# Seven products for one of four first-layer column groups in blocks 3 to 6 of a retention and MLP kernel, with x sums on GpSimd

## The chip, the cores and the metric

The kernel runs on one core of a Trainium2 chip. The metric is the device time of one execution in microseconds (us). A profiled execution gives a trace beside its time: its span is the time between its first and last instruction. Engines are called PE (matmuls), ACT, DVE, POOL (GpSimd) and SP, whose queue issues most DMAs here.

## The reference

For 8 batches of 8 heads, 576 positions and head size 64, the kernel computes a retention layer and then a two-layer MLP on all 4608 tokens.

```python
scores = scale * q @ k.T                       # per batch and head
ret = scores * where(rel >= 0, gamma[h] ** rel, 0)
x = (ret @ v)  ->  [4608, 512]                 # heads side by side
h = x @ w_in                                   # 512 -> 2048
g = gelu_tanh(h)
out = g @ w_out                                # 2048 -> 512, float32
```

## The kernel before, in words

**Tiling.** The MLP runs in nine blocks of 512 tokens: block t (0 to 7) is the first 512 positions of batch t, and block 8 holds the last 64 positions ("tails") of all batches. Each block has a first layer (512 to 2048 columns, hidden chunks f = 0 to 15 of 128 each) and a second layer. While block t runs, pieces of the retention of batch t+1 are placed between its matmuls, and batch t+2 is loaded and cast.

**First layer.** In most blocks it is sixteen calls of `up` (L474): four matmuls of 128x512 (L480) fill one PSUM bank `hp`, and ACT writes its gelu to `gT` in float16 (L486). `act_sums` (L634) then forms, on DVE, the sums s1, s2, s4 and an in-place difference of parts of `gT`; they are the left sides of the second layer.

**Second layer.** It is always done by Strassen and Winograd's scheme: seven half-size products (`prod`, L648), each in two halves of eight 128x256 matmuls, in the order 1, 6, 5, 7, 2, 4, 3. Products 6, 7 and 4 add to one bank `opB`. `after` (L672) takes the results out: product 1 by an ACT copy (s1, tag k1), product 6 by a DVE add (u2, tag k2), product 7 by another (u3, tag k3). Product 7 may write `opB` only when the u2 add has read it.

**Seven products in the first layer.** In blocks 7 and 8 (`WIN`), three of four column groups of the first layer are done in the same way by `up_prod` (L554): group j holds the hidden chunks 2j, 2j+1, 8+2j and 9+2j, and seven products of four 128x256 matmuls (L574) replace four `up`. Products 1, 6, 7 and 4 add up in one bank hB, 5 and 3 in hC, 2 goes to hA. Between them the partial sum of hB is copied out: after product 1 by ACT (L594), after product 6 by ACT (L600), after product 7 by DVE (L602). DVE adds hA or hC to the copies (L581), and ACT takes the gelu of the sums; that gelu is recorded after the next product or `up`. The sums of weights come from `in_sums` (L518) and those of x from `x_sums` (L535), all on DVE, the latter kept in x12 and x34. Their tiles take places of the loads' ring.

**What sets the order.** Everything is emitted in program order; `at(t, u, f)` places a piece of work f behind step u (0 to 29) of block t. Steps 0 to 15 are the first layer; 16 to 29 are the fourteen halves of the second. In blocks 2 to 6 the scores of chunks 0 and 1 of the next batch (and of tails, where there are any) are at step 11 or 9, the outputs `outs` of those chunks at 15, of chunks 2 and 3 at 24. `outs` ends in `state` (L402), which multiplies the casts of k and v of chunks 0 and 1 of the batch after, and in `put` (L466), the ACT copy to xT. `later` (L784) is a DVE scan and a `spread` (L430), two ACT copies of 64x256; two of them stand at the start of each block.

**Loads.** `pump` issues loads in a fixed list on SP as buffers of one ring of 16 come free; a mark in the list holds it until `resume` at step 29. A batch is twelve loads of 256 KB, in the order k, q, v for chunks 0 to 3, followed by six tail loads (two each for k, q and v) for batches 4, 5 and 7. From step 16 the casts are placed: k and q on POOL (L275), v on ACT (L262) or, for batch 3, POOL. `gate` (L979), a one-element POOL copy that reads the last s4, stands ahead of them. One step behind the casts stand two DMA transposes of k and q (L308) and, with tails, two POOL casts and one more transpose (`cast_tails`, L245).

Of the kernel before, what the change touches and what calls it, by code (L numbers as in the profile page):

```python
# [20 lines left out]
def kernel(  # L21
# [23 lines left out]
    LD = 16  # L45
# [3 lines left out]
    NT4 = 4  # L49
    scale = 1.0 / math.sqrt(D)  # L50
# [18 lines left out]

    def lds():  # L70
        return sb.tile([128, 512], F32, tag="ld", name="ld", bufs=LD)

# [66 lines left out]
    q_ld = {"next": 0, "free": LD, "hold": False}  # L139

    def pump(freed=0):
        q_ld["free"] += freed
        while q_ld["next"] < len(seq) and not q_ld["hold"]:
            s = seq[q_ld["next"]]
            if s[0] == "h":
                q_ld["hold"] = True
                q_ld["next"] += 1
                return
            if s[0] != "t":
                if q_ld["free"] == 0:  # L150
                    return
                q_ld["free"] -= 1
            q_ld["next"] += 1
            {"b": load, "i": load_w_in, "o": load_w_out, "t": load_tails}[s[0]](*s[1:])
# [101 lines left out]
    def cast(b, key, c, eng):  # L256
        a = att[b]
        raw = a["raw"].pop((key, c))
        dst = a[key][:, 512 * c : 512 * c + 512]
        if key == "v":  # L260
            if eng is nc.scalar:
                eng.copy(out=dst, in_=raw)  # L262
            else:
                eng.tensor_copy(out=dst, in_=raw)
        elif b < NPE:
            y = c % 2
            eng.tensor_tensor(
                out=a[key][:, 1024 * (c // 2) : 1024 * (c // 2) + 1024].rearrange("p (n l d) -> p l n d", l=2, d=D)[:, y],
                in0=raw.rearrange("p (n d) -> p n d", d=D),
                in1=sp[key][:, :, y].unsqueeze(2).to_broadcast([128, 8, D]),  # L270
                op=ALU.mult,
            )
        else:
            s0 = {"q": 0, "k": 2}[key] + (b >= PAIR)
            eng.tensor_tensor(  # L275
                out=dst.rearrange("p (h d) -> p h d", d=D),
                in0=raw.rearrange("p (h d) -> p h d", d=D),
                in1=sc[:, s0].unsqueeze(2).to_broadcast([128, 8, D]),
                op=ALU.mult,
            )  # L280
# [233 lines left out]
    WIN = {t: 3 for t in (NTB - 2, NTB - 1)}  # L514
    GW = max(WIN.values())
    wi = {}

    def in_sums(j, ns):  # L518
        if not wi:
            for g in range(0, GW, 2):  # L520
                for n in "234":
                    wi[n, g // 2] = sb.tile([128, 2, 512], F16, tag="ld", name="wi" + n, bufs=LD)
# [12 lines left out]
    def x_sums(t):  # L535
        if not xw:
            for n in ("12", "34"):
                x = sb.tile([128, 2, 4, 2, TL], F16, tag="ld", name="x" + n, bufs=LD)
                xw[int(n[0])], xw[int(n[1])] = x[:, 0], x[:, 1]
            for n in range(3):  # L540
                for s in "svu" if n < 2 else "vu":
                    wk[s, n] = sb.tile([128, 512], F32, tag="ld", name="w" + s, bufs=LD)
# [3 lines left out]
        for s, x, y, f in (  # L546
# [3 lines left out]
            nc.vector.tensor_tensor(out=s, in0=x, in1=y, op=f)  # L550

    wk, wb, due = {}, {}, []

    def up_prod(t, j, m):  # L554
# [23 lines left out]
        s, v, u3 = wk["s", j % 2], wk["v", j % 3], wk["u", j % 3]  # L578
# [55 lines left out]
    def act_sums(t, f0, f1, us=slice(0, 2), parts=(0, 1)):  # L634
# [6 lines left out]
        if 0 in parts:  # L641
            nc.vector.tensor_tensor(out=s["1"], in0=a21, in1=a22, op=ALU.add)  # L642
            nc.vector.tensor_tensor(out=s["2"], in0=s["1"], in1=a11, op=ALU.subtract)
            nc.vector.tensor_tensor(out=a21, in0=a11, in1=a21, op=ALU.subtract)  # L644
        if 1 in parts:
            nc.vector.tensor_tensor(out=s["4"], in0=a12, in1=s["2"], op=ALU.subtract)  # L646
# [25 lines left out]
    def after(t, m, u):  # L672
# [87 lines left out]
    def cast_w(kind, *i):  # L760
# [11 lines left out]
        pump(1)  # L772
# [4 lines left out]
    def cc(b, key, c, eng):  # L777
        cast(b, key, c, eng)
        pump(1)
# [135 lines left out]
    for t, b in TP.items():  # L915
        at(t, 3, lambda b=b: tail_values(b))
# [30 lines left out]
    for t in range(1, B):  # L947
        b, tl = t + 1, TP.get(t)
        s0, o0, s1, o1 = U2 if t == 1 else (11 if t in (2, 3) else 9, 15, 15, 24)
# [6 lines left out]
        else:  # L956
            at(t, s1, lambda b=b: (score(b, 2), score(b, 3)))
            at(t, 17, lambda b=b: masks(b, 2))
            at(t, 19, lambda b=b: masks(b, 3))
# [7 lines left out]
    for b in range(NPE, B):  # L967
# [23 lines left out]
    for t in range(NTB):  # L991
# [9 lines left out]
        else:  # L1001
# [7 lines left out]
            todo = deque(f + h for f in range(2 * WIN.get(t, 0), NH) for h in (0, NH))  # L1009
            for w in (W_ORDER if t in WIN else ()):  # L1010
# [7 lines left out]
                def token(w):  # L1018
# [5 lines left out]
                    elif w[0] in "ab":  # L1024
                        act_sums(t, 2 * int(w[1]), 2 * int(w[1]) + 2, parts=("ab".index(w[0]),))
                    else:
                        up_prod(t, int(w[0]), int(w[1]))
                steps.append((mixed, 0 if w[:1] in ("a", "b", "Q") else 1 if w else 2))
            for f in range(0 if t == 1 or t in WIN else NH):
# [55 lines left out]
```

## Time and profile before

| what | us |
|---|---|
| median of three runs (lowest to highest) | 293.72 (293.19 to 295.14) |
| profiled execution, time and span | 293.76 and 292.0 |
| start of blocks 2, 3, 4, 5, 6, 7 on PE | 84.43, 114.70, 145.15, 175.60, 205.37, 236.00 |
| PE busy in block 4 (145.15 to 175.60) | 30.45 of 30.45 |
| DVE, ACT and POOL busy in block 4 | 18.92, 18.84, 9.11 |
| PE busy over the span | 280.1 |

A row of a timeline reads: start in us, duration in us, engine, line, operation, output and inputs with their shape and type, how many in a row; the bracket is the idle time of the engine ahead of it, and what ended that. A row of the chain of waits reads: start, duration, engine, output, line. The granted clock of PE was 1.00 in each of these blocks.

### The profile page before, as it was taken

What the parts mean: (1) busy time and instruction counts of PE and PEld (TensorE: products, weight loads), DVE (VectorE), ACT (ScalarE), POOL (GpSimd) and SP (SyncE); (2) the same over time, 40 slices, a digit from 0 to 9 for tenths busy, and PEclk for the clock granted to TensorE, in tenths of its full rate; (3) what the DMA queues carried; (4) which work ended last, traced back from release to release, by engine and by line L of the source; (5) the groups of instructions that cost most, each with busy time, mean ns of one, the idle gap of its engine ahead of it and who ended that gap; (6) DMA issues with size and microseconds to landing.
All of it is one profiled execution on the core that took longest, in us unless ns stands there. A gap on an engine that the chain in (4) does not pass through costs nothing.

```text
span 292.0 us, 7383 instructions
## 1 busy us (share of the span) xinstructions
PE 280.1 (96%) x3024; PEld 207.6 (71%) x3024; DVE 204.1 (70%) x409; ACT 169.8 (58%) x321; POOL 100.0 (34%) x128
## 2 busy tenths in 40 slices
PE   6889998999999999999999999999999999999993
PEld 2558877888874687468845884488548887887783
DVE  7796998666864874477548834784489968974863
ACT  5487754987249545964396647664666258507810
POOL 4589779910661175008500730068030000000000
PEclk9999999999999999999999999999999999999998
DMA  6999999989999999999999979997952030003013
GB/s 195 308 382 370 364 293 228 252 213 163 225 192 230 235 206 183 244 235 210 200 267 209 218 147 270 216 190 99 271 95 38 2 144 3 0 21 125 3 36 108
DMA packets 139585, 53.95 MB, mean 185 GB/s; under 512 B 118048, under 2 KB 131360, under 8 KB 139552
## 3 DMA queue, kind: packets, MB, share of 16 engines
q1 hardware_dynamic: 138960, 52.97, 80.4%
q8 instruction: 23, 0.38, 0.6%
q10 hardware_dynamic: 592, 0.52, 0.5%
q14 instruction: 10, 0.08, 0.1%
HBM read 36.70 MB, written 9.44 MB: 158 GB/s over the span
## 4 chain that ended last, share of the span: by engine, by line
PE 66%; SPq 8%; DMA 8%; ACT 5%; POOL 5%; DVE 5%; issue 1%; POOLq 0%; DVEq 0%; ACTq 0%
PE hp L480 18%; PE opB L665 11%; PE opA L665 8%; PE opC L665 7%; SPq L101 5%; DMA ld<-in_moe_w_in_dram 4%; PE hp L501 4%; PE hB L574 3%; SPq L96 3%; ACT gT L486 3%; PE xs L459 2%; POOL w_out_sb L771 2%; PE st L383 2%; DMA ld<-in_v_dram 2%; DMA ld<-in_q_dram 2%; PE hC L574 2%
## 5 line engine op out<-in xcount | busy, mean ns | idle before, releaser
L480 PE MATMUL hp<-xT,w_in_sb 128*128 128x512 f16 x352 | 79.1, 379 | 0.6 <-ACT xT L469 0.3
L486 ACT ACTIVATE gT<-hp 128x512 f16<-128x512 f32 x88 | 50.1, 600 | 22.6 <-PE hp L480 22.0
L480 PEld LDWEIGHTS <-w_in_sb 128*128 128x128 f16 x352 | 34.0, 98 | 39.0 <-issue 1.1
L665 PEld LDWEIGHTS <-gT 128*128 128x128 f16 x576 | 54.9, 98 | 8.9 <-issue 0.9
L665 PEld LDWEIGHTS <-s 128*128 128x128 f16 x432 | 42.2, 98 | 4.9
L642 DVE TENSOR_TENSOR s<-gT 128x512 f16<-128x512 f16 x36 | 15.6, 434 | 31.2 <-ACT gT L486 24.5
L665 PE MATMUL opA<-w_out_sb,gT 128*128 128x256 f16 x288 | 36.0, 273 | 0.6 <-ACT w_out_sb L771 0.4
L392 DVE TENSOR_TENSOR ret<-st,cm 128x512 f16<-128x512 f32 x48 | 30.2, 681 | 3.6 <-PE st L383 3.6
L469 ACT CAST xT<-xs 128x512 f16<-128x512 f32 x36 | 19.2, 590 | 20.4 <-PE xs L459 17.0
L501 PE MATMUL hp<-xT,w_in_sb 128*128 128x256 f16 x256 | 29.9, 273 | 0.9 <-POOL w_in_sb L771 0.5
L275 POOL TENSOR_TENSOR ck<-ld,sc 128x512 f16<-128x512 f32 x24 | 25.0, 1043 | 9.7 <-DMA ld<-in_k_dram 9.7
L501 PEld LDWEIGHTS <-w_in_sb 128*128 128x128 f16 x256 | 24.3, 98 | 5.2 <-POOL w_in_sb L771 2.3
L434 ACT CAST tbd<-ws 64x256 f16<-64x256 f32 x48 | 19.4, 403 | 14.8 <-DVE ws L425 14.2
L275 POOL TENSOR_TENSOR cq<-ld,sc 128x512 f16<-128x512 f32 x24 | 26.1, 1088 | 2.6 <-DMA ld<-in_q_dram 2.1
L665 PE MATMUL opB<-wt,gT 128*128 128x256 f16 x224 | 26.8, 273 | 0.0
L979 POOL COPY gate<-s 128x1 f16<-128x1 f16 x5 | 0.9, 190 | 74.6 <-DVE s L646 74.6
L262 ACT CAST cv<-ld 128x512 f16<-128x512 f32 x24 | 14.2, 618 | 17.2 <-DMA ld<-in_v_dram 17.1
L508 ACT ACTIVATE gT<-hp 128x512 f16<-128x512 f32 x32 | 18.3, 605 | 3.5 <-PE hp L501 3.3
L679 DVE TENSOR_TENSOR k<-k,opB 128x512 f32<-128x512 f32 x17 | 11.7, 686 | 11.7 <-PE opB L665 10.7
L644 DVE TENSOR_TENSOR gT<-gT 128x512 f16<-128x512 f16 x36 | 18.0, 499 | 0.0
L665 PE MATMUL opB<-wt,s 128*128 128x256 f16 x144 | 17.4, 273 | 0.0
L665 PE MATMUL opC<-wt,s 128*128 128x256 f16 x144 | 17.2, 272 | 0.0
(122 smaller groups left out, 406.4 us busy)
## 6 DMA issues: line engine op xcount, KB each, us to landing
ld<-in_q_dram SPq DMA_DIRECT2D x32, 256.0 KB, 5.2
ld<-in_k_dram SPq DMA_DIRECT2D x32, 256.0 KB, 5.1
ld<-in_v_dram SPq DMA_DIRECT2D x32, 256.0 KB, 5.3
out_dram<-ost SPq DMA_DIRECT2D x16, 512.0 KB, 3.9
ld<-in_moe_w_in_dram SPq DMA_DIRECT2D x16, 256.0 KB, 5.7
ld<-in_moe_w_out_dram SPq DMA_DIRECT2D x16, 256.0 KB, 5.6
lt<-in_k_dram SPq DMA_DIRECT2D x8, 128.0 KB, 4.7
lt<-in_q_dram SPq DMA_DIRECT2D x8, 128.0 KB, 4.4
```

The source lines that it names most:

```text
L101: nc.sync.dma_start(out=t.rearrange("p (h d) -> p h d", d=D), in_=src[b, :, 128 * c : 128 * c + 128, :].rearrange("h s d -> s h d"),)
L275: eng.tensor_tensor(out=dst.rearrange("p (h d) -> p h d", d=D), in0=raw.rearrange("p (h d) -> p h d", d=D), in1=sc[:, s0].unsqueeze(2).to_ ...
L392: nc.vector.tensor_tensor(out=r.rearrange("p (n i) -> p n i", i=128), in0=t.rearrange("p (n i) -> p n i", i=128), in1=(cm if b < PAIR else ...
L434: cp(out=(tbd[b % 2][r, c, :, r] if c < NC - 1 else tbt[b % NT4][r, :, r]), in_=w[r])
L469: nc.scalar.copy(out=xT[:, g0 : g0 + 2], in_=xs.rearrange("p (n g t) -> p g n t", n=HP, g=2))
L480: nc.tensor.matmul(hp.rearrange("p (g t) -> p g t", t=TL), w_in_sb[:, ct, 128 * fc : 128 * fc + 128], xT[:, o : o + TB // TL, ct, :], star ...
L486: nc.scalar.activation(out=gT[t][:, fc].rearrange("p i n -> p (i n)"), in_=hp, func=AF.Gelu_apprx_tanh)
L501: nc.tensor.matmul(hps[n][:, 256 * x : 256 * x + 256].rearrange("p (g t) -> p g t", t=TL), w_in_sb[:, ct, 128 * (fs[n] + x) : 128 * (fs[n] ...
L508: nc.scalar.activation(out=gT[t][:, f : f + 2, 2 * u : 2 * u + 2, :].rearrange("p f i n -> p f (i n)"), in_=hp.rearrange("p (f n) -> p f n ...
L642: nc.vector.tensor_tensor(out=s["1"], in0=a21, in1=a22, op=ALU.add)
L644: nc.vector.tensor_tensor(out=a21, in0=a11, in1=a21, op=ALU.subtract)
L665: nc.tensor.matmul(op[tag][:, HD * u : HD * u + HD], lhs(f), rhs[:, f], start=(new and f == 0), stop=(f == NH - 1), skip_group_check=True,)
```

## The change

Blocks 3 to 6 (`MID`) now do column group 0 (chunks 0, 1, 8, 9) by seven products. The order of their first layer is written out: four plain `up`, then products and plain `up` in turn. The pieces c and d in it are the sums s1 and s2 and the in-place difference, which `act_sums` now makes separately; s4 of all chunks is made in two DVE ops of 1024 elements behind product 6 of the second layer. `in_sums` of group 0 moves to steps 17 and 18 of block 2; for groups 1 and 2 it stays in block 6. `x_sums` of blocks 3 to 6 runs on POOL at step 0 of the block.

Because the tiles of these sums live from block 2 on, the ring of 16 buffers is split in two rings of 8, `ld` and `lm`. Loads up to batch 3 alternate between them; from batch 4 on they have the 8 of `ld` alone, so that the loads 9 to 12 of a batch wait for casts of its first loads. The first of the three work tiles of each kind takes the tags k1, k2 and k3 of the second layer.

Steps move as well. In blocks 3 to 6 the scores go to step 12, the outputs to 17 and 25, the masks of chunks 2 and 3 to 19 and 21, the cast of the tails' v from 3 to 16, and the casts, `gate` and the transposes of the batch after (blocks 3 to 5) by four steps. In block 7 one plain `up` comes first.

```diff
-    LD = 16
+    LD = 8
+    FIRST = 3
...
-                if q_ld["free"] == 0:
+                tag = "ld" if s[0] == "b" and s[1] >= FIRST + 1 else ("ld", "lm")[q_ld["n"] % 2]
+                if q_ld["free"][tag] == 0:
...
+    MID = {t: 1 for t in range(FIRST, NTB - 2)}
...
-            nc.vector.tensor_tensor(out=s, in0=x, in1=y, op=f)
+            (nc.gpsimd if t in MID else nc.vector).tensor_tensor(out=s, in0=x, in1=y, op=f)
...
+        for n in parts:
+            for o, x, y, f in (
+                ((s["1"], a21, a22, ALU.add), (s["2"], s["1"], a11, ALU.subtract)),
+                ((s["4"], a12, s["2"], ALU.subtract),), ((a21, a11, a21, ALU.subtract),),
+            )[n]:
+                eng.tensor_tensor(out=o, in0=x, in1=y, op=f)
...
             for f in range(0, NH if t in WIN else 0, 2):
                 act_sums(t, f, f + 2, parts=(1,))
+            for f in range(0, NH if t in MID else 0, 4):
+                act_sums(t, f, f + 4, parts=(1,))
...
+    M_ORDER = "    01 c11 02 05 d11  06  07  04  c21 03 d21   c01 d01   c31 d31".split(" ")
     for n in range(GW):
-        at(NTB - 3, 17 + 2 * n, lambda n=n: in_sums(n, (3, 2)))
-        at(NTB - 3, 18 + 2 * n, lambda n=n: in_sums(n, (4, 1)))
-    at(NTB - 3, 27, lambda: x_sums(NTB - 2))
+        t, u = (FIRST - 1, 17 + 2 * n) if n < 1 else (NTB - 3, 15 + 2 * n)
+        at(t, u, lambda n=n: in_sums(n, (3, 2)))
+        at(t, u + 1, lambda n=n: in_sums(n, (4, 1)))
+    for t in MID:
+        at(t, 0, lambda t=t: x_sums(t))
+    at(NTB - 3, 29, lambda: x_sums(NTB - 2))
...
-        at(t, 3, lambda b=b: tail_values(b))
+        at(t, 16 if t in MID else 3, lambda b=b: tail_values(b))
...
-        s0, o0, s1, o1 = U2 if t == 1 else (11 if t in (2, 3) else 9, 15, 15, 24)
+        s0, o0, s1, o1 = U2 if t == 1 else (12, 17, 17, 25) if t in MID else (11 if t == 2 else 9, 15, 15, 24)
...
+        if t0 in MID:
+            ut = [u + 4 for u in ut]
...
+                    elif w[0] in "cd":
+                        f = 2 * int(w[1])
+                        act_sums(t, f, f + 2 * int(w[2]), parts=({"c": 0, "d": 2}[w[0]],))
```

In `M_ORDER` an empty entry is the next plain `up` (chunks 2, 10, 3, 11, 4, 12, ...), 01 to 07 are products 1 to 7 of group 0, c and d the sums, whose first digit is the group.

More of the change, by code (lines that the diff above doesn't have):

```diff
@@ L138, with pump @@
             seq.append(("h",))
-    q_ld = {"next": 0, "free": LD, "hold": False}
-    def pump(freed=0):
-        q_ld["free"] += freed
+    q_ld = {"next": 0, "n": 0, "tag": None, "free": {"ld": LD, "lm": LD}, "hold": False}
+    def pump(raw=None):
+        if raw is not None:
+            q_ld["free"][ring.pop(id(raw))] += 1
         while q_ld["next"] < len(seq) and not q_ld["hold"]:
@@ L518, in in_sums @@
     def in_sums(j, ns):
[L519 to L522, printed above, removed]
+        for n in "234":
+            if (n, j // 2) not in wi:
+                wi[n, j // 2] = kept("wi" + n, [128, 2, 512], F16, "lm" if j < 2 else "ld")
         c, lo, hi = slice(256 * (j % 2), 256 * (j % 2) + 256), slice(256 * j, 256 * j + 256), slice(DF // 2 + 256 * j, DF // 2 + 256 * j + 256)
@@ L577, in up_prod, with work @@
                 )
-        s, v, u3 = wk["s", j % 2], wk["v", j % 3], wk["u", j % 3]
+        def work(s):
+            n = j % (2 if s == "s" else 3)
+            if n == 0 and m == {"s": 1, "v": 6, "u": 7}[s]:
+                wk[s, 0] = sb.tile([128, 512], F32, tag=KT[s], name=KT[s], bufs=1)
+            return wk[s, n] if (s, n) in wk else None
+        s, v, u3 = work("s"), work("v"), work("u")
         def add(o, a, b):
@@ L771, in cast_w @@
         eng(out=dst, in_=src)
-        pump(1)
+        pump(src)
     HALF = (2, 6)
```

48 lines of the change are left out of this document (26 added, 22 removed).

## The prediction

> **What bounds the kernel now.** I read the page first, then the chain that ended last, then the timelines of block 4 engine by engine.
>
> ```profile
> PE 280.1 (96%) x3024; PEld 207.6 (71%) x3024; DVE 204.1 (70%) x409; ACT 169.8 (58%) x321; POOL 100.0 (34%) x128
> ```
>
> PE is busy 96% of the span. From 114.7 us on, the chain of waits is nearly all PE work, with hardly a wait in it:
>
> ```profile
> 145.31 8.63 PE hp L480 x40
> ...
> 238.34 0.44 PE hA L574 x4
> 238.78 0.86 PE hp L480 x4
> ```
>
> Forty plain matmuls take 8.63 us, so an `up` (four of 512 columns) is 0.863 us; a product (four of 256) is 0.437. PE starts blocks 2 to 7 at 84.43, 114.70, 145.15, 175.60, 205.37 and 236.00: whatever makes PE wait in blocks 2 to 6 is added to the time. So I looked at what the products wait for. ACT at the start of block 4 (start = 145.15):
>
> ```profile
> 146.27 0.60 ACT L486 ACTIVATE gT<-hp 128x512 f16<-128x512 f32 x1 [1.45 <-PE hp L480]
> 146.90 0.82 ACT L434 CAST tbd<-ws 64x256 f16<-64x256 f32 x2
> 147.74 0.60 ACT L486 ACTIVATE gT<-hp 128x512 f16<-128x512 f32 x1
> 148.36 0.82 ACT L434 CAST tbd<-ws 64x256 f16<-64x256 f32 x2
> 149.20 1.09 ACT L486 ACTIVATE gT<-hp 128x512 f16<-128x512 f32 x2
> ```
>
> ACT lags: the four spreads lie between the gelus, and the fourth gelu ends at start+5.14, while PE has done four `up` at +3.45. DVE's activation sums wait for that gelu:
>
> ```profile
> 150.32 0.42 DVE L642 TENSOR_TENSOR s<-gT 128x512 f16<-128x512 f16 x1 [3.03 <-ACT gT L486]
> 150.78 0.42 DVE L643 TENSOR_TENSOR s<-s,gT 128x512 f16<-128x512 f16 x1
> 151.12 0.42 DVE L644 TENSOR_TENSOR gT<-gT 128x512 f16<-128x512 f16 x1
> ```
>
> Last, what GpSimd does to DVE, in block 6 (POOL runs two tail casts there) and in block 2:
>
> ```profile
> 213.64 2.48 POOL L275 TENSOR_TENSOR e<-lt,sc 128x512 f16<-128x512 f32 x2 [10.49 <-DMA lt<-in_k_dram]
> ```
>
> ```profile
> 213.60 0.42 DVE L643 TENSOR_TENSOR s<-s,gT 128x512 f16<-128x512 f16 x1
> 213.94 1.26 DVE L644 TENSOR_TENSOR gT<-gT 128x512 f16<-128x512 f16 x1
> 215.13 1.26 DVE L646 TENSOR_TENSOR s<-gT,s 128x512 f16<-128x512 f16 x1
> ```
>
> ```profile
> 101.65 1.23 DVE L425 TENSOR_TENSOR ws<-vs,gt 128x256 f32<-128x256 f32 x1
> 102.81 1.28 DVE L392 TENSOR_TENSOR ret<-st,cm 128x512 f16<-128x512 f32 x2
> 104.38 0.69 DVE L679 TENSOR_TENSOR k<-k,opB 128x512 f32<-128x512 f32 x1 [0.29 <-ACT k L718]
> ```
>
> Beside POOL a sum of two SBUF tiles takes 1.2 us instead of 0.42; the masks, which read PSUM, keep 0.64.
>
> **The change part by part.** The sum is made against the profiled execution: 293.76 us, of which 292.0 is span and 1.76 lies around it (0.04 above the median of 293.72).
>
> *PE work.* In each of four blocks 4 `up` (3.45) become 7 products (3.06): 4 x 0.39 = 1.57 us less.
>
> *The products' waits on ACT.* Products 1, 6, 7 and 4 add up in one bank, hB; between them the partial sum is copied away. In the changed program's order, product 6's weight load waits for ACT's copy of product 1, product 7's for ACT's copy after product 6. ACT's order is gelu, spreads, gelu, spreads, gelu, gelu, copy 1, gelu of copy 1 plus hA, gelu of the fifth `up`, copy 6. Times from block start, by the rows above: fourth gelu 5.14; copy 1 (0.58) ends 5.67, so product 6, wanted at 4 x 0.863 + 3 x 0.437 + 0.863 = 5.63, slips 0.1. DVE does two activation sums ahead of the hA add: from 5.17, third slot at 5.97 (the 151.12 row), add 0.69, done 6.66. The gelu behind it starts at 6.7 (0.63), the next one at 7.24, copy 6 at 7.78, which ends near 8.37; product 7 starts at 8.42 instead of 6.93. So 1.5 us of PE wait per block. Bounds: 1.0 if the DVE add were ready at once, 2 if ACT's ops don't overlap as in these rows. Taken 4 x 1.5 = 6.0.
>
> *The banks behind them.* The eleventh `up` takes the bank of the ninth, whose gelu stands behind the gelu of copy 6 plus hC; that add stands behind the sums of the second group. From the end of the eighth `up`: 0.16 + gelu 0.6 + two sums 0.85 + add 0.69 + gelu 0.63 + gelu 0.55 = 3.48, while PE asks after 0.437 + 2 x 0.863 + scores 0.78 (0.55 in block 5, without tails) = 2.94 (2.71). 0.5 us per block, 0.75 in block 5: 2.25; bounds 0 and 4.
>
> *Weight sums on DVE in block 2.* Four `in_sums` ops now stand ahead of the u2 add, which product 7 of the second layer (the fourth in its order, wanted at 105.84) waits for, since both use opB. POOL is casting then. Alone they take 4 x 0.38 and the add ends at 106.45: 0.6 of wait. Beside POOL the first two end at 104.0 and 105.2, masks at 106.4, two more by 107.2, the add by 107.9: 2.1. POOL casts in the whole stretch (to 105.79, again from 106.89), so I take 2.1, less the 0.34 us that PE waited before block 3 anyway: 1.8; bounds 0.3 and 2.7. In block 6 POOL is idle and the add comes in time: nothing.
>
> The Trainium skill, SBUF — State Buffer, "Who interferes with whom", says the same of the pair: a DVE instruction with two SBUF inputs waits for a GpSimd instruction that reads SBUF, one with a PSUM input does not. By a rule of that kind it is free where POOL is between loads, which would put block 2 nearer its lower bound; the rows alone give the 1.8.
>
> *The late gate.* s4 moves behind product 6 as two 1024-wide ops (block 8's row: four 512-wide in 1.42 us), and `gate` on POOL waits for it. With t6 the end of product 6: u2 add from t6+0.27, s4 done t6+2.3; then eight casts of 1.04 on POOL, before: done 8.4 us after the gate at 162.36. Behind the gate stand: the casts, loads 9 to 12 of the next batch (only 8 buffers left, so they wait for casts), tail loads, both transposes, ett, the output send and the next eight loads on SP, the tail casts and x sums on POOL. Covers: PE's `state` needs the k casts of chunks 0 and 1, ready t6+5.7, asked at t6 + 3 x 1.75 + 1.05 = t6+6.3, a cover of 0.6. Transposes start near the next block's +1 and land by +10; scores ask after +13 (they were moved from slot 11 or 9 to 12). v casts end before the next block's first gelu. So nothing, with 0 to 1 a block as bounds. Output sends, tail v casts (now slot 16) and masks have PE work of over 2 us before them.
>
> *x sums on POOL.* Four ops per block; no row has f16 sums there, the nearest is the 1.04 of the casts (bounds 0.6, a plain POOL copy, and 1.25). Before block 3 the tail casts end at 117.24, product 5 wants x1 at about 120: hidden. In blocks 4 and 6 the chain runs block t6 at 22.2, gate 24.5, casts to 33, tail casts (tail loads are issued after load 12; they landed 5.7 and 5.2 us after issue at 137.82 and 139.61) to 35.3 or 36, x1 one us later, against a block of 32.2 and product 5's need 4.3 later: ready 4.1 to 4.8, wait 0 to 0.5. But the x sums then run beside DVE's two sums at 5.17, which end at about 7.2 instead of 6.05: 1.2 us more on the chain to product 7. 2 x 1.2 = 2.4; bounds 0 and 5 (tail loads later). Block 5 has no tail casts: nothing.
>
> Sum: -1.57 + 6.0 + 2.25 + 1.8 + 2.4 = +10.9, so 304.6 us.
>
> **The rivals.**
> 1. *Light:* the two-engine collisions are missed: blocks 2, 4 and 6 pay 0.3 in all instead of 4.2. 300.7. For it: POOL has gaps (1.1 us before the third k cast in block 2). Against: the 1.26 rows.
> 2. *Heavy:* the gate chain becomes the bound: tail loads land 2 us later, product 5 waits in blocks 4 and 6 and `state` in all four (0.5 each): 304.6 + 2 + 2 = 308.6. For it: loads were paced by DMA in every block (1.1 us each on SP's queue). Against: the DMA share should fall when issue waits for casts.
> 3. *Other side:* products 6 and 7 find their copies done. Place: ACT between fourth gelu and copy 6. It decides at start+6.9: if ACT's spreads went elsewhere or the hA add came 1.5 us sooner, the change would give its 1.57: 292.2. For it: in block 7 of before, the same copies cost PE nothing. Against: there ACT has no spreads and DVE no sums ahead; here the program's order has both.
>
> **How the numbers follow.** Forecast (main case, 302.5 to 306.5) 0.52; light 0.23; heavy 0.10; other side 0.07; half of the ACT stall (about 297) 0.08. Range 298 to 309 leaves out the other side and the edges. A measurement of this kernel can tell about 1% (2.9 us) from no change. Faster by over 1% (below 290.8) is in no case: 0.02; within 1% the other side and a part of the half case: 0.11; slower 0.87.
>
> **What would show it.** Right: PE rows of product 7 (hB <- x, wi) in blocks 3 to 6 with about 1.5 us idle before them, released by an ACT copy; opB in block 2 released by DVE near 108; the u2 add at 107; two DVE sums of over 1 us at the start of blocks 4 and 6; blocks of 32 us. Wrong: no idle PE before hB, blocks of 30.1 us; or idle before hC (product 5), released by POOL, or before us, which would be the heavy case.

## The result and the profile after

The changed kernel takes 308.2 us (median of four executions, 305.90 to 311.98) where the kernel before, measured beside it, takes 293.5: a ratio of 1.046, 95% interval [1.036, 1.057]. Ratios here leave out an execution that is over 1.5% above the fastest of its kernel, in this case the one of 311.98 us. The profiled execution took 305.90 us with a span of 304.1, against 293.76 and 292.0 before. The prediction was 304.6, range 298 to 309, slower.

The page's first part, after the change:

```profile
PE 281.8 (93%) x3072; PEld 212.9 (70%) x3072; DVE 215.5 (71%) x417; ACT 172.9 (57%) x329; POOL 119.4 (39%) x144
```

PE's busy time hardly moved (280.1 before), the span is 12.1 us longer: PE waits. The waits of PE, summed over the run (line of the waiting instruction, what released it, us in total, times, longest):

```profile
PE hB L589 <- ACT k L621: 7.0, 5, 2.1
PE opB L686 <- DVE k L700: 2.8, 2, 2.6
...
PE hp L492 <- ACT gT L498: 1.2, 3, 0.4
```

These are the three waits that the prediction named: product 7 behind ScalarE's copy, product 7 of the second layer behind the u2 add, the eleventh plain group behind a bank. Two small ones in these rows were not named: 0.6 us before hB in block 7, and 0.21 before opB in block 6, where the prediction had the add come in time. By blocks, from the first PE instruction of one to that of the next (block 7 with all that follows):

| | 2 | 3 | 4 | 5 | 6 | 7, 8 and end |
|---|---|---|---|---|---|---|
| before | 30.27 | 30.45 | 30.45 | 29.77 | 30.63 | 56.04 |
| after | 34.20 | 32.06 | 32.78 | 30.88 | 33.21 | 56.87 |

Block 4 (start 150.34) shows the chain. PE, then ScalarE, VectorE and GpSimd on the timeline (start, duration, engine, line, what; in brackets the idle time before it and its releaser):

```profile
155.10 1.03 PE L492 MATMUL hp<-xT,w_in_sb 128*128 128x512 f16 x4
155.96 0.60 PE L589 MATMUL hB<-x,wi 128*128 128x256 f16 x4
156.40 1.03 PE L492 MATMUL hp<-xT,w_in_sb 128*128 128x512 f16 x4
159.35 0.61 PE L589 MATMUL hB<-x,wi 128*128 128x256 f16 x4 [1.92 <-ACT k L621]
```

```profile
154.22 1.09 ACT L498 ACTIVATE gT<-hp 128x512 f16<-128x512 f32 x2
155.20 0.59 ACT L615 COPY k<-hB 128x512 f32<-128x512 f32 x1
157.70 0.63 ACT L606 ACTIVATE gT<-k 128x512 f16<-128x512 f32 x1 [1.91 <-DVE k L602]
158.24 0.58 ACT L498 ACTIVATE gT<-hp 128x512 f16<-128x512 f32 x1
158.72 0.58 ACT L621 COPY k<-hB 128x512 f32<-128x512 f32 x1
```

```profile
155.34 0.44 DVE L667 TENSOR_TENSOR s<-gT 128x512 f16<-128x512 f16 x1 [2.08 <-ACT gT L498]
155.81 1.26 DVE L667 TENSOR_TENSOR s<-s,gT 128x512 f16<-128x512 f16 x1
157.00 0.67 DVE L602 TENSOR_TENSOR k<-k,hA 128x512 f32<-128x512 f32 x1
```

```profile
154.35 1.15 POOL L564 TENSOR_TENSOR x<-x,xT 128x512 f16<-128x512 f16 x1
155.46 1.33 POOL L564 TENSOR_TENSOR x<-xT 128x512 f16<-128x512 f16 x1
```

Read it backwards from the wait. Product 7 (159.35) waits for the copy of 158.72; that copy is third in ScalarE's queue behind the gelu of 157.70, which waited 1.91 us for the hA add of 157.00. The hA add was possible at 155.8, when the copy of product 1 was done; it stood behind two activation sums, and the second of these took 1.26 us beside GpSimd's x sum of 155.46. ScalarE stands idle from 155.79 to 157.70, until after PE has asked for product 7 (156.40 + 0.863 = 157.26).

Block 2: first the table of windows (length, then busy time and instructions of PE, PE's weight loads, VectorE, ScalarE and GpSimd, the granted clock, the DMA share and GB/s), then VectorE's and PE's timelines.

```profile
105.00:108.80 3.80, 1.19 (x11) 0.92 (x10) 3.80 (x7) 0.72 (x2) 3.14 (x3) 1.00 1.01 224
108.80:112.30 3.50, 3.50 (x20) 2.49 (x18) 1.63 (x4) 0.52 (x1) 2.08 (x2) 0.52 1.00 194
112.30:118.00 5.70, 5.70 (x81) 5.11 (x80) 1.80 (x4) 2.98 (x6) 3.40 (x4) 0.99 1.32 163
```

```profile
106.35 1.26 DVE L543 TENSOR_TENSOR w_in_sb<-w_in_sb 128x512 f16<-128x512 f16 x1
107.54 0.67 DVE L700 TENSOR_TENSOR k<-k,opB 128x512 f32<-128x512 f32 x1
```

```profile
108.26 2.94 PE L686 MATMUL opB<-wt,gT 128*128 128x256 f16 x16 [2.61 <-DVE k L700]
```

VectorE is busy for all of the first window, PE for a third of it. What comes behind was not predicted: just after PE goes on at 108.26, the granted clock falls to half for 3.4 us, and sixteen matmuls take 2.94 us that take 1.91 in the other blocks. So block 2 loses 3.93 us. PE wanted opB at 103.74 + 1.75 = 105.49 and got it 2.77 later; 0.34 that it waited at the block's end before is gone; and from opB to the end of the block it takes 10.02 us where the kernel before takes 8.52 without that wait: 1.50 for the clock.

### The profile page after: what moved, and what is told of

Read it like the earlier page. It is cut to its first block, busy times and chain, and to the rows that moved or that the text cites. A ratio compares the mean times of both kernels' runs of the same rounds, so it can differ in the third digit from the quotient of the medians.

```text
span 304.1 us, 7542 instructions
## 1 busy us (share of the span) xinstructions
PE 281.8 (93%) x3072; PEld 212.9 (70%) x3072; DVE 215.5 (71%) x417; ACT 172.9 (57%) x329; POOL 119.4 (39%) x144
## 5 line engine op out<-in xcount | busy, mean ns | idle before, releaser
L492 PE MATMUL hp<-xT,w_in_sb 128*128 128x512 f16 x288 | 68.4, 379 | 1.2 <-ACT gT L498 1.2
L686 PEld LDWEIGHTS <-gT 128*128 128x128 f16 x576 | 56.1, 99 | 13.3 <-issue 3.9
L498 ACT ACTIVATE gT<-hp 128x512 f16<-128x512 f32 x72 | 41.0, 601 | 20.2 <-PE hp L492 19.9
L492 PEld LDWEIGHTS <-w_in_sb 128*128 128x128 f16 x288 | 28.0, 98 | 27.5 <-issue 1.2
L686 PE MATMUL opB<-wt,gT 128*128 128x256 f16 x224 | 27.8, 279 | 2.8 <-DVE k L700 2.8
L287 POOL TENSOR_TENSOR ck<-ld,sc 128x512 f16<-128x512 f32 x24 | 26.1, 1086 | 6.9 <-DMA ld<-in_q_dram 3.6
L513 PEld LDWEIGHTS <-w_in_sb 128*128 128x128 f16 x256 | 24.4, 98 | 4.3 <-POOL w_in_sb L794 1.1
L589 PEld LDWEIGHTS <-wi 128*128 128x128 f16 x120 | 11.1, 97 | 13.7 <-ACT k L621 8.4
L606 ACT ACTIVATE gT<-k 128x512 f16<-128x512 f32 x20 | 12.6, 630 | 13.6 <-DVE k L602 13.4
L520 ACT ACTIVATE gT<-hp 128x512 f16<-128x512 f32 x32 | 18.3, 604 | 3.3 <-PE hp L513 3.2
L589 PEld LDWEIGHTS <-w_in_sb 128*128 128x128 f16 x160 | 15.6, 98 | 4.4
```

The source lines that it names most:

```text
L287: eng.tensor_tensor(out=dst.rearrange("p (h d) -> p h d", d=D), in0=raw.rearrange("p (h d) -> p h d", d=D), in1=sc[:, s0].unsqueeze(2).to_ ...
L492: nc.tensor.matmul(hp.rearrange("p (g t) -> p g t", t=TL), w_in_sb[:, ct, 128 * fc : 128 * fc + 128], xT[:, o : o + TB // TL, ct, :], star ...
L498: nc.scalar.activation(out=gT[t][:, fc].rearrange("p i n -> p (i n)"), in_=hp, func=AF.Gelu_apprx_tanh)
L513: nc.tensor.matmul(hps[n][:, 256 * x : 256 * x + 256].rearrange("p (g t) -> p g t", t=TL), w_in_sb[:, ct, 128 * (fs[n] + x) : 128 * (fs[n] ...
L520: nc.scalar.activation(out=gT[t][:, f : f + 2, 2 * u : 2 * u + 2, :].rearrange("p f i n -> p f (i n)"), in_=hp.rearrange("p (f n) -> p f n ...
L589: nc.tensor.matmul(pb[:, 256 * i : 256 * i + 256].rearrange("p (g t) -> p g t", t=TL), w(kt, i), x(kt), start=(new and i == kt == 0), stop ...
```

## The experiments

Twelve kernels. Blocks in us from the profiled execution of each, ratio to the kernel before with its 95% interval:

| run | time | ratio | blocks 2, 3, 4, 5, 6 |
|---|---|---|---|
| weight sums late | 308.0 | 1.050 [1.045, 1.055] | 29.95, 35.36, 33.77, 30.88, 34.62 |
| x sums on VectorE | 311.9 | 1.064 [1.058, 1.070] | 34.61, 33.01, 34.70, 31.87, 35.46 |
| spreads late | 306.7 | 1.047 [1.043, 1.051] | 32.54, 31.76, 33.22, 30.87, 34.21 |
| plain groups, same schedule | 295.9 | 1.010 [1.006, 1.013] | 29.77, 30.45, 30.45, 29.77, 32.02 |
| all three moved | 298.1 | 1.016 [1.011, 1.021] | 29.77, 31.75, 31.74, 30.03, 31.92 |
| and the add first | 296.8 | 1.009 [1.006, 1.012] | 29.77, 31.07, 31.08, 29.80, 31.62 |
| and spreads later still | 294.7 | 1.0035 [1.001, 1.006] | 29.77, 30.55, 30.54, 29.52, 30.90 |
| and blocks 6, 7 | 294.1 | 1.0025 [1.0004, 1.0047] | 30.16, 30.54, 30.54, 29.53, 30.29 |
| order alone | 297.6 | 1.0145 [1.009, 1.020] | 33.19, 30.41, 30.29, 29.69, 32.18 |
| order and late weight sums | 294.0 | 1.001 [0.999, 1.003] | 29.77, 30.41, 30.30, 29.70, 30.07 |
| kernel before, gap of 4 sums | 297.8 | 1.010 [1.005, 1.016] | 34.86, as before from 3 to 5 |
| kernel before, gap of 8 sums | 301.7 | 1.027 [1.024, 1.030] | 37.94, as before from 3 to 5 |

### One part undone at a time

**Weight sums late.**

```diff
-        t, u = (FIRST - 1, 17 + 2 * n) if n < 1 else (NTB - 3, 15 + 2 * n)
+        t, u = (FIRST - 1, 23 + 2 * n) if n < 1 else (NTB - 3, 15 + 2 * n)
```

> The changed kernel, but the four weight sums of block 2 stand on VectorE behind the adds after product 7 instead of ahead of the u2 add. Theory (collision and what follows it): PE's 2.61 us idle before opB at 108.26 goes, and with it the lowered granted clock that came behind it (0.66 from 108 to 111, 0.77 from 111 to 114); block 2 falls from 34.2 us to 30.3, the span by 3.9 to about 300.2, the time to about 302.0. Rival A (the clock dips by itself, the gap is only the wait): the span falls by 2.6 and 0.64 to 0.77 stays in the windows near 110. Rival B (the smaller load ring and the later gate pace the blocks): block 2 gets shorter but a later wait takes it back, time within 1 us of 305.9.

Measured: block 2 does what the theory says (no gap, 29.95), and the time stays. But not for rival B's reason. Block 3 of this run (start 115.18), VectorE, then PE:

```profile
120.36 1.41 DVE L667 TENSOR_TENSOR s<-gT 128x512 f16<-128x512 f16 x1 [3.23 <-ACT gT L498]
121.81 1.26 DVE L667 TENSOR_TENSOR s<-s,gT 128x512 f16<-128x512 f16 x1
122.99 0.67 DVE L602 TENSOR_TENSOR k<-k,hA 128x512 f32<-128x512 f32 x1
```

```profile
125.34 1.03 PE L589 MATMUL hB<-x,wi 128*128 128x256 f16 x4 [3.01 <-ACT k L621]
```

Both sums are stretched now, in blocks 3, 4 and 6, and product 7 waits 3.01, 2.90 and 2.89 us instead of 1.19, 1.92 and 2.10. In block 3 GpSimd's x sums follow the tail casts, and these wait for their load:

```profile
115.71 2.33 POOL L287 TENSOR_TENSOR e<-lt,sc 128x512 f16<-128x512 f32 x2 [2.61 <-DMA lt<-in_k_dram]
...
121.45 1.33 POOL L564 TENSOR_TENSOR x<-xT,x 128x512 f16<-128x512 f16 x1
```

The load does not come earlier because PE does: the x sums end at 122.78, start+7.6, where in the changed kernel they end at start+3.2. The gap in block 2 had kept them apart from the sums of block 3. And behind the 3.01 us wait the clock falls again (0.51 from 125.3 to 128.7). A wait removed upstream was paid back downstream, twice.

**x sums on VectorE.**

```diff
-            (nc.gpsimd if t in MID else nc.vector).tensor_tensor(out=s, in0=x, in1=y, op=f)
+            nc.vector.tensor_tensor(out=s, in0=x, in1=y, op=f)
```

> The changed kernel with the x sums of blocks 3 to 6 on VectorE instead of GpSimd, at the same place in the program. Theory (collision): the activation sum of 1.26 us at the start of blocks 4 and 6 goes back to 0.42, PE's idle before product 7 (hB<-x,wi) falls from 1.92 and 2.10 to about 1.2 in these two, blocks 3 and 5 stay, so 1.6 us less, span about 302.5. Rival (x sums are dear wherever they stand, as VectorE is the late engine at a block's start): product 7 waits as long or longer in all four blocks, time 306 or more.

Measured: the rival. The x sums cost only 0.42 each on VectorE, but at the block's start they stand ahead of the scans, whose results ScalarE's spreads wait for, and the gelus queue behind the spreads. Block 5, ScalarE (start 187.08):

```profile
188.21 0.60 ACT L498 ACTIVATE gT<-hp 128x512 f16<-128x512 f32 x1 [2.05 <-PE hp L492]
189.81 0.82 ACT L446 CAST tbd<-ws 64x256 f16<-64x256 f32 x2 [1.00 <-DVE ws L437]
```

From there all of ScalarE is 1.0 us late, and PE now also waits before product 6: 0.82 in blocks 3 and 5, 2.17 and 2.44 in blocks 4 and 6, where the tail casts stretch the x sums too.

**Spreads late.**

```diff
-                at(t + 1, c, lambda c=c, nb=b + 1: later(nb, c))
+                at(t + 1, c, lambda c=c, nb=b + 1: scan(nb, c))
+                at(t + 1, c + 9 if t + 1 in MID else c, lambda c=c, nb=b + 1: spread(nb, c, A.copy))
```

> The changed kernel with ScalarE's four spreads at the start of blocks 3 to 6 (two pairs of 0.82 us) moved behind the copies that the products wait for; the scans on VectorE stay. Theory (ScalarE's chain of gelus, spreads and copies is what product 7 waits for): the fourth gelu ends 1.64 us earlier, PE's idle before product 7 falls from 1.19, 1.92, 1.18 and 2.10 to 0, 0.3, 0 and 0.5, so 5 to 5.6 us less, less at most 1.6 where the moved spreads delay the gelu that frees the eleventh bank: span 298.5 to 301. Rival (loads and gate pace the blocks): blocks 3 to 6 keep their 31 to 33 us, time within 1 us of 305.9.

Measured: block 3's wait falls from 1.19 to 0.36; blocks 4, 5 and 6 keep 1.79, 1.18 and 1.92. So ScalarE was not the only thing in the way. Block 5 shows why, VectorE and GpSimd (start 182.10):

```profile
186.38 1.25 DVE L667 TENSOR_TENSOR s<-gT 128x512 f16<-128x512 f16 x1 [1.16 <-ACT gT L498]
187.66 0.42 DVE L667 TENSOR_TENSOR s<-s,gT 128x512 f16<-128x512 f16 x1
188.00 0.68 DVE L602 TENSOR_TENSOR k<-k,hA 128x512 f32<-128x512 f32 x1
```

```profile
186.19 1.15 POOL L564 TENSOR_TENSOR x<-xT,x 128x512 f16<-128x512 f16 x1
```

The gelu is done 0.82 us earlier, at start+4.25, the sum starts 0.83 earlier and thereby meets the last x sum; it takes 1.25 instead of 0.43 and ends at start+5.53, to 0.01 us where it ended before. The gain went wholly into the collision. Block 2 is 1.66 us shorter than in the changed kernel although its gap is the same 2.61: here the clock stayed at 1.00 behind it; the last section shows why.

**Plain groups, same schedule.** All sixteen first-layer groups of blocks 3 to 6 are computed plainly; the ring in two tags, the moved steps and the late gate stay.

```diff
-    M_ORDER = "    01 c11 02 05 d11  06  07  04  c21 03 d21   c01 d01   c31 d31".split(" ")
+    M_ORDER = "    c01 d01     c11 d11     c21 d21     c31 d31".split(" ")
...
-            todo = deque(f + h for f in range(2 * {**WIN, **MID}.get(t, 0), NH) for h in (0, NH))
+            todo = deque(f + h for f in range(2 * WIN.get(t, 0), NH) for h in (0, NH))
```

> The changed kernel with all sixteen first-layer groups of blocks 3 to 6 plain again (no products, no x sums there, weight sums back in block 6), but with everything else of the change kept: the ring split in two tags of 8, from the fourth batch on only one of them, the moved steps, the fourth sums behind product 6 and with them the later gate. Theory (the loss is in the products' waits, the collisions and the gap of block 2): blocks 2 to 6 go back to 30.3 to 30.6 us, time 293.5 to 294.5, the same as before the change. Rival (smaller ring and later gate cost something of themselves): blocks of 31 us or more with PE waiting for state, scores or av, time 296 or more.

Measured, one line of the table of windows per block, 2 to 6 (length first):

```profile
85.54:115.31 29.77, 29.77 (x287) 20.27 (x284) 19.32 (x38) 17.97 (x36) 12.48 (x13) 1.00 1.07 212
115.31:145.76 30.45, 30.45 (x311) 21.02 (x308) 18.08 (x36) 18.43 (x35) 8.85 (x10) 1.00 1.01 192
145.76:176.21 30.45, 30.45 (x311) 21.01 (x308) 18.45 (x36) 19.65 (x37) 10.46 (x12) 1.00 0.91 196
176.21:205.98 29.77, 29.77 (x287) 20.29 (x284) 16.96 (x34) 17.76 (x34) 8.37 (x10) 1.00 1.02 196
205.98:238.00 32.02, 30.62 (x294) 20.90 (x292) 22.33 (x48) 16.87 (x32) 4.74 (x5) 1.00 0.52 114
```

PE is busy for the whole of blocks 2 to 5, and blocks 3 to 5 are as long as before to the hundredth: the smaller ring and the later gate cost nothing there. The heavy rival also had product 5 wait for late x sums, which this kernel does not make; for these it is the changed kernel's own trace that speaks, which lists no wait of PE before hC, us or st in blocks 3 to 6. Together they end the heavy rival. Block 6 is 1.4 longer (PE waits 0.88 for the u2 add and 0.38 for a mask, behind the twelve weight sums that stand there in this kernel), and what follows is 0.7 longer (0.8 in the changed kernel): block 7's x sums and order were changed too, and PE waits 0.5 there before hB. That makes 1.6 with the 0.5 that block 2 is shorter; the rest of the 2.7 us of span is this execution's start, 1.1 us later at block 2, and starts vary by as much between the runs shown.

### The cure, and what it is worth

**All three moved:** weight sums late, spreads late, and the x sums on VectorE behind the scans (step 2 instead of 0).

> Three edits at once to the changed kernel: weight sums of block 2 behind the adds after product 7, the spreads of blocks 3 to 6 behind the copies, and the x sums of blocks 3 to 6 on VectorE behind the two scans instead of on GpSimd. Each alone gave nothing, since the collision of VectorE and GpSimd took it back; theory (both at once must be taken away): no sum of 1.2 us at the start of a block any more except beside the tail casts of blocks 4 and 6; fourth gelu ends at start+4.25, sums 4.6 to 5.45, hA add 6.05, copy 7.8, so product 7 waits 0.8 in blocks 3 and 5, up to 1.2 in 4 and 6, block 2 has no gap: span 297 to 299, time 299 to 301. Rival (the three lie on different chains and do not add up, or the x sums on VectorE push scans and copies back as in the run with x sums at the block's start): time 305 or more.

Measured 298.1, a little better than the theory's 299 to 301. No stretched sum is left before the hA add, product 7 waits 0.35 to 0.42 in all four blocks, the eleventh group 0.77 in three. What single moves did not give, the three give together.

**And the add first:**

```diff
-    M_ORDER = "    01 c11 02 05 d11  06  07  04  c21 03 d21   c01 d01   c31 d31".split(" ")
+    M_ORDER = "    01 02 05 c11 d11  06   07  04 c21  03 d21  c01 d01   c31 d31".split(" ")
```

> The run before it, and two edits more: in blocks 3 to 6 the two activation sums stand behind the hA add instead of ahead of it, with one plain group more between product 6 and product 7 (product 7 then wanted at start+7.8), and the x sums of block 7 stand again two steps earlier in block 6, as before the change. Theory (the order of sums and copies is all that is left): copy after product 6 done at 7.2, no idle before product 7 in blocks 3 to 6, at most 0.5 before the eleventh plain group; block 7's wait of 0.6 goes: blocks of 30.1 to 30.6 us, time 292 to 295, the kernel before or up to 1.5 us less. Rival (the waits only move on to a bank or to the gelus further back): blocks of 31 us or more, time 296 or more.

Measured 296.8: the theory's part on product 7 holds (no wait), its block lengths do not. The spreads, put off, now stand as four in a row (125.53, 1.63 us) ahead of the gelus that free the banks of the tail scores, and PE waits there: 0.23 and 0.28 by the list of waits, and from the first score to the next plain group block 3 takes 1.65 us, against 0.77 before. The wait had moved on, as the rival said.

**And spreads later still** (`c + 13` instead of `c + 9`).

> The run with the add first, x sums on VectorE and weight sums late, where PE lost 0.88 at the tail scores of each block to the gelus behind ScalarE's four spreads; here the spreads stand four steps later, behind these gelus. Theory: the tail scores wait no more, blocks 3, 4 and 6 fall by 0.5 to 0.9 (31.07 to 30.2), block 5 stays within 0.2 of 29.8: span 292.5 to 294, time 294.3 to 295.5, the kernel before within 1%. Rival (the gelus are late by themselves, since ScalarE has the copies of the products on top): the scores wait as before, time 296.5 or more; or the spreads are late now for the xs products behind them, and PE waits there.

Measured 294.7: the scores wait no more, and the profile lists no wait of PE in blocks 2 to 5. Yet block 3 takes 30.55, not 30.2. Its first layer with the scores takes 14.45 us against 14.70 before the change, but then the first opB starts 4.25 us behind the first opA, against 3.89 in the order-alone run below. By the trace it is released by ScalarE's copies to xT, which stand behind the spreads now and come 0.37 later for it. This is the rival's second part, the spreads late for what stands behind them.

**And blocks 6 and 7:** the second and third group's weight sums behind the u2 add (`20 + 2 * n` instead of `15 + 2 * n`), block 7's order as before the change.

> The run before it, and blocks 6 and 7 as they can be had: the weight sums of the second and third group in block 6 behind the u2 add, and the order of block 7 as in the kernel before the change. Theory: block 6 loses its waits of 0.32 and 0.21 before xs and opB, block 7 its 0.5 before hB and the 0.3 of the moved group; what is left of the change is four times 0.26 us of PE work: span 290.5 to 292, time 292.3 to 294, 0 to 0.6% faster than before, at the edge of what can be measured. Rival (the products' copies on ScalarE and VectorE cost as much elsewhere as PE saves): time 294.5 or more.

Measured 294.1, ratio 1.0025 [1.0004, 1.0047]: at the rival's edge, and not faster. The weight sums now hold up block 7's first add, and PE waits 0.74 there.

**Order alone:** only the `M_ORDER` line above, in the changed kernel.

> The changed kernel with one edit: in blocks 3 to 6 the two activation sums stand behind the hA add instead of ahead of it, and one plain group more stands between product 6 and product 7. The x sums stay on GpSimd, the spreads at the block's start, the weight sums of block 2 ahead of the u2 add. Theory (what product 7 waits for is the hA add behind two sums, whatever makes these late): the add starts when the copy after product 1 is done, start+5.5, the copy after product 6 ends near 7.9, product 7 is wanted at 7.8: its waits of 1.19, 1.92, 1.18 and 2.10 fall to 0.1 to 0.3 in all four blocks, although the sums still take 1.26 beside GpSimd; span near 298, time 298 to 301 with the gap of block 2 and its clock still there. Rival (GpSimd's x sums or ScalarE's spreads must go as well): product 7 still waits 1 us or more in blocks 4 and 6, time 303 or more.

Measured 297.6. After this one line no wait before product 7 is listed in blocks 3 to 6. Block 4 (start 147.33), VectorE and PE:

```profile
152.81 0.69 DVE L602 TENSOR_TENSOR k<-k,hA 128x512 f32<-128x512 f32 x1 [2.70 <-ACT k L615]
153.41 0.42 DVE L667 TENSOR_TENSOR s<-gT 128x512 f16<-128x512 f16 x1
153.87 1.26 DVE L667 TENSOR_TENSOR s<-s,gT 128x512 f16<-128x512 f16 x1
155.05 0.41 DVE L667 TENSOR_TENSOR gT<-gT 128x512 f16<-128x512 f16 x1
155.89 0.69 DVE L623 COPY k<-hB 128x512 f32<-128x512 f32 x1 [0.43 <-PE hB L589]
```

```profile
153.39 1.89 PE L492 MATMUL hp<-xT,w_in_sb 128*128 128x512 f16 x8
155.18 0.61 PE L589 MATMUL hB<-x,wi 128*128 128x256 f16 x4
155.62 1.03 PE L492 MATMUL hp<-xT,w_in_sb 128*128 128x512 f16 x4
156.64 0.60 PE L589 MATMUL hB<-xT,wi 128*128 128x256 f16 x4
```

```profile
154.54 0.58 ACT L621 COPY k<-hB 128x512 f32<-128x512 f32 x1
```

The collision is still there (the 1.26 us), GpSimd still does the x sums, ScalarE still the spreads first; but nobody on the way to product 7 stands behind the stretched sum.

The line does two things, though: it puts the sums behind the add, and it puts one plain group more between products 6 and 7. No run does one without the other, but the rows tell them apart. The copy after product 6 (154.54, the last row above) ends at start+7.93, 7.79, 7.89 and 7.79 in blocks 3 to 6, where in the changed kernel it ends at 8.25, 8.96, 8.22 and 9.14. So the sums ahead of the add cost 0.3 us in blocks 3 and 5, and 1.2 and 1.35 in blocks 4 and 6, where one of them is stretched. At its old place, wanted at start+6.92, product 7 would by these rows still wait 0.9 to 1.1 us for the copy (7.79 to 7.93, and 0.05 to its start); the plain group more, 0.86 us, covers that, and 0.05 to 0.2 are left. In a block without a collision most of the wait is thus ScalarE's chain with one plain group too few to cover it, and the sums are a quarter; with a collision they are over half.

**Order and late weight sums:** the order line alone, with the weight sums of blocks 2 and 6 late, and block 7 as before the change.

> The run with only the order mended (adds ahead of the sums, one plain group more before product 7; x sums on GpSimd and spreads at the block's start, as in the change), with the weight sums of block 2 behind the adds after product 7, those of block 6 behind the u2 add, and block 7's x sums and order as before the change. Theory (order and weight sums are the whole loss; spreads and x sums then cost nothing where they are): block 2 near 30, blocks 3, 4 and 5 at 30.4, 30.3 and 29.7 as in the order run, block 6 near 30.9, no clock drop; span 291 to 292.5, time 292.8 to 294.3, with the kernel before within 0.3%. A gain of over 1% is in neither theory: four blocks save at most 4 x 0.39 us. Rival (late x sums on GpSimd hold back sums and gelus once block 2 is 4 us shorter, as they did in the run with the weight sums alone): blocks 3, 4 and 6 at 31 or more, time 295.5 or more.

Measured 294.0, ratio 1.001 [0.999, 1.003]; blocks 2 to 5 have no wait, no clock drop. From the start of block 2 to that of block 7 it takes 150.25 us where the kernel before takes 151.57, a gain of 1.3, but only 0.26 of it in blocks 3 to 5, where by the plain-groups run only the products and their order tell; it gives 1.0 back in block 7, where PE waits 0.81 before hB behind VectorE's late sums. None of these kernels beats the one before.

### The clock behind a gap

The kernel before the change, with four or eight sums into a tile that nobody reads, on VectorE ahead of the u2 add of block 2:

```diff
+    at(2, 17, lambda: more(n // 2))
+    at(2, 18, lambda: more(n - n // 2))
```

> The kernel before the change, with four sums of two w_in_sb slices into a spare tile that nobody reads, on VectorE ahead of the u2 add of block 2, where the changed kernel has its weight sums; nothing else of the change. Theory (the gap alone takes the clock down, in some executions): PE idle of 2.0 to 2.6 us before opB, and in a part of the executions a granted clock of 0.5 for 3.4 us after it, which costs 1.7: times in two groups, about 295.5 to 296 and 297.2 to 297.7, with mean clocks 0.006 apart. Rival (the low clock belongs to something else in the change): all times 295.5 to 296, clock as in the kernel before.

> The same with eight such sums. Theory: beside GpSimd's casts they take 5 to 8 us, PE idle of 5 to 7 us before opB, longer than 3.4, and the granted clock goes to 0.5 behind it in every execution: the gap plus 1.7 us, time 300 to 302.5, all mean clocks 0.994 or lower. Rival (the low clock belongs to something else in the change): the gap alone, 298.5 to 300, granted clock 1.00 behind it.

Measured with eight: a gap of 6.61 us (105.62 to 112.23), one window in it and one behind it:

```profile
108.60:112.20 3.60, 0.00 (x0) 0.00 (x0) 3.50 (x6) 0.62 (x1) 2.26 (x2) 0.50 1.07 214
112.20:115.80 3.60, 3.57 (x20) 2.66 (x20) 1.40 (x3) 0.00 (x0) 2.09 (x2) 0.59 1.32 197
```

All four executions have a mean clock of 0.989 (0.996 to 1.000 in those of the kernel before), and block 2 takes 37.94 us instead of 30.27. Nothing of the change is in this kernel, so the half clock belongs to the gap. With four sums the profiled execution (299.99 us) has a gap of 3.26 us and 0.50 behind it; the others have mean clocks of 0.991 (298.09 us) and 1.00 (295.17 and 297.41). A gap of this length brings the half clock or not; the last section shows what decided it in the traces. The two groups of times that were forecast do not show: the two at full clock lie 2.2 us apart, and why is open.

## Why the prediction was right, and where its sizes were off

The sum was +10.9 against the profiled execution, measured +12.1. The median of 308.2 lies 3.6 us above the forecast, above the main case (302.5 to 306.5), near the upper end of the range, and next to the heavy rival's 308.6; it is the places of the waits that decide for the main case. The mechanism was the one named; the terms:

| step of the prediction | predicted | measured |
|---|---|---|
| PE work, four blocks | -1.57 | -0.9 |
| product 7 behind the copies | 4 x 1.5 = 6.0 | 4 x 1.35 = 5.4 |
| x sums beside the sums, blocks 4 and 6 | 2.4 | 1.7 |
| eleventh plain group's bank | 2.25 | 3 x 0.48 = 1.4, none in block 5 |
| weight sums ahead of the u2 add, block 2 | 1.8 | 2.4 |
| clock behind that gap | not named | 1.5 |
| late gate and ring | 0 | 0 |
| block 7 | 0 | 0.8 |
| start, to block 2 | 0 | -0.35 |

That the two totals lie so close is in part luck: the three terms of waits in blocks 3 to 6 were taken 2.1 us too large and the saving on PE 0.7 too large, while 2.3 us (the clock, block 7) were not in the sum at all and block 2 was 0.6 short.

The measured column is read from starts, not from the idle figures, which count from a modelled end: product 7 was wanted at start+6.92 (the `up` of start+6.06 and 0.863) and came at start+8.31, 9.01, 8.27 and 9.19 in blocks 3 to 6, so 1.35 to 1.39 late without a collision and 2.09 and 2.27 with one. PE work is what is left: blocks 3 to 6 grew by 7.63 in all, product 7's slips are 7.10, the banks' 1.44.

**PE work** was taken from the matmul rows alone. The term left out is the third wait on bank hB: product 4 waits for VectorE's copy after product 7. In block 3 of the changed kernel it was wanted at 127.04 + 0.863 = 127.90 and came at 128.05; it is 0.15 in each of the four blocks, 0.6 of the 0.7 that are missing. In the order-alone run, where nothing waits long, block 4's first layer with its scores takes 14.51 us against 14.69 before: 0.18 less instead of 0.39. Its rows show where the rest is: the copy of 155.89 ends at 156.58, so product 4, wanted at 156.48, starts at 156.64, and product 7 slips 0.06. Blocks 3 and 5 of that run are only 0.04 and 0.08 shorter than before the change; the best seen is the 0.25 of the run with the spreads later still. Seven products of which four share a bank, with copies between them, kept between a tenth and two thirds of what they save.

**The products' waits** were right in place, releaser and nearly in size. Block 5, where no sum ahead of the add is stretched, follows the working link by link: copy of product 1 done at start+5.55 (5.67 in the prediction), hA add at 6.59 (6.66), copy after product 6 at 8.22 (8.37).

**The collisions** came in blocks 4 and 6 as forecast, one sum of 1.26 in each, worth 0.74 and 0.92 against the 1.2 that was taken for two. That block 3 was called hidden was true only because of the gap of block 2, as the first experiment showed: with block 2 cured, block 3 collides too and loses 1.8 more. This dependence was not in the prediction. The Trainium skill, SBUF — State Buffer, "Who interferes with whom", agrees as to which instructions are hit: those of VectorE with two SBUF inputs took up to 1.42 beside GpSimd, adds with a PSUM input kept 0.67 to 0.69. Not each one is hit: the sum of 155.34 took 0.44 though an x sum ran until 155.50.

**Block 2** is the step that was mis-sized most: its gap was at the upper bound (2.77, bounds to 2.7), and the clock behind it was not thought of. Executions of the changed kernel at 305.90, 306.39 and 310.02 us have mean clocks of 0.993, 0.994 and 0.979; a drop of 3.4 us to half speed is 0.0056 of this span. So the third fits two drops more, behind other waits; only the first has a trace, and for the third this is not shown.

**The rivals.** Light fell with the 1.26 rows, heavy with the plain-groups run and the changed kernel's list of waits. Half of the ACT stall fell with 1.35 us in a block without a collision. The other side's condition (spreads elsewhere, or the hA add 1.5 us sooner) was not enough by itself: with the spreads late product 7 still comes 0.53 late in block 3, and with the add first as well the copy after product 6 ends at start+7.07, still behind the 6.92 at which the change's order asks for product 7. The waits go only with the plain group more, and the gain is then 0.25 us a block at best instead of 0.39.

## What to carry to other kernels

When a product's partial sum is copied away between products, look in program order at what stands ahead of that copy on each engine of the chain: here two sums that nobody needed soon, placed one line too early, cost 0.3 to 1.35 us a block, in all twice what the products could save. Then count what PE has to do over that chain: one plain group between products 6 and 7 was too little, two were nearly enough. Repair the order first: that one line took the time from 308.2 to 297.6 us (in the traces 6.4 us in blocks 3 to 6, and 1.0 in block 2, where the clock stayed at 1.00 this time), while weight sums, x sums and spreads, moved one at a time, gave nothing that lasts, because each gain ran into the next collision or wait. A saving of 0.39 us in 30 that needs three engines to be in step is soon gone.

## What the runs showed of the hardware

**The granted clock behind a gap of PE.** In the traces it falls to half for 3.41 us at a time (twice that behind the gap of 6.61), and the stretches at full clock between are whole multiples of 3.413 us: in the changed kernel 102.40 and 191.15 us, 30 and 56 times. So the clock is set in steps of 3.413 us. Cut at these steps, the block 2 of the changed kernel (the first two rows) and that of the spreads-late run (the last two) differ, though the gap is 2.61 us in both; PE's busy time is the first figure behind the comma, the clock is the number behind the five engines:

```profile
105.55:108.96 3.41, 0.80 (x8) 0.62 (x7) 3.41 (x6) 0.36 (x2) 2.59 (x3) 1.00 1.00 217
108.96:112.37 3.41, 3.41 (x19) 2.42 (x17) 1.54 (x3) 0.36 (x1) 2.08 (x2) 0.50 0.99 194
```

```profile
104.36:107.77 3.41, 1.79 (x17) 1.47 (x15) 3.41 (x5) 1.27 (x3) 3.15 (x3) 1.00 0.99 195
107.77:111.18 3.41, 2.42 (x23) 2.17 (x23) 2.61 (x5) 0.62 (x1) 2.64 (x4) 1.00 1.05 224
```

In the first, one step holds the whole gap, and the next one runs at half. In the second, the gap is cut in two, 1.62 and 0.99 us, and the clock stays. The gaps of 1.9 us and more in blocks 2 to 6 of all traces, by what PE idled in the step that has most of the gap (ends of matmuls are modelled):

| clock in the next step | idle in one step (the gap) |
|---|---|
| half | 2.15 (2.17), 2.61 (2.61), 2.79 (3.26), 2.88 (3.01), 3.26 (3.26), 3.41 and 2.69 (6.61) |
| full | 2.01 (3.26), 2.00 (2.44), 1.93 (2.89), 1.92 (1.92), 1.72 (2.90), 1.62 (2.61), 1.59 (2.10), 1.56 (1.92) |

So not the length of the gap decides here, but how much of one step it fills: 2.15 us of 3.41 was enough, 2.01 was not, and nothing lies between. Where the steps fall differs between executions, and so the gap of 2.61 us cost 1.5 us in one and nothing in the other. The cost, from opB to the end of block 2, is 1.5 us in the changed kernel and with four sums, and 1.2 with eight, where over half of the time at half clock fell into the gap itself.

The Trainium skill, TensorE: Matmul & The Clock Gate, "What's actually happening", gives the clock as half or full and the deciding window as free-running and 3413 ns long. These traces agree with that; but that the clock falls only behind a whole idle window of about 3.4 us, as its table has it, does not hold here.
